# A scheduler that searches its priorities: 1,000 rounds of shifted keys, dearer key loads, and sums of w_in made early

## The chip, the cores and the metric

The kernel runs on one core of a Trainium2 chip. Its five engines each work through an instruction stream of their own: PE (TensorE: matmuls; PEld is its loading of weights), DVE (VectorE), ACT (ScalarE), POOL (GpSimd) and SP (SyncE), which here does nothing but issue DMAs. Streams wait for each other by semaphores. The metric is the device time of one execution in microseconds (us), the median of several runs.

## The reference

Sliding-window attention is followed by a two-layer network with a squared rectifier. There are B = 8 sequences of S = 576 tokens, H = 8 heads of D = 64, and a window of 32 tokens to either side:

```
scores = where(|i - j| <= 32, q k^T / 8, -1e9)
attn   = softmax(scores) v                      # (8, 8, 576, 64)
x      = attn, heads side by side               # (4608, 512)
h      = x @ w_in                               # w_in  (512, 2048)
out    = (s * relu(h)^2 + b) @ w_out            # w_out (2048, 512)
```

Everything comes in and goes out as float32; s and b are single numbers.

## The kernel before

**The work.** Attention goes through units of 128 keys. For each pair of heads PE makes the scores (L847), ACT takes the exponential (L875), DVE multiplies by the band mask (L879), PE multiplies by v (L905), and DVE divides by the sum (L927, L929) into a tile `xn`. PE (L936) or, from unit 24 on, a DMA (L953) turns `xn` into `XT`, the input of the first layer with its features on the partitions. One PE task, an attention step, holds the products with v of one unit and the scores of the next.

The first layer (`s1`) goes through blocks m of tokens (the first 512 tokens in m 0 to 2, the next 1024 in four blocks of 256, m 3 to 6, then m 7 to 12 of 512) and groups f of 128 hidden features. PE adds up 4 products per group into one of two banks `W` (L1192), ACT rectifies into a tile `r1` (L1199), and DVE squares two groups at once into `GT` (L1207). The second layer (`second`, L1358) works on 512 tokens at a time with seven products of half size in place of eight. For that DVE makes sums of the squares (`total`, L1350) and once, from w_out, four sums of weights (`weight_sums`, L1330). DVE combines the products into the output tiles (L1374), and SP stores them (L1383). The constant b is put in by way of column sums of w_out: PE makes four of them (`constant`, L1435, r = 0 to 3), one for each quarter of w_out, the last one once the last part of w_out is cast (L599).

For the last two full blocks of 512 tokens, 5 pairs of feature groups (features 6 to 15 of 16) use seven products too (`quad_group`, L1276). These need four sums each of w_in (L1239): `quad_sums` makes those of the first four pairs in the tiles `NAT` and those of the fifth in the tiles of the exponentials, all late.

**The packets.** From sequence 3 on, `later` loads q and k of a sequence as a packet of three parts (`piece`): q of 512 tokens (L773), k of 512 tokens in four DMAs (L780), and the tails, tokens 512 to 575 of both. They land in the ring `stg`, POOL (ACT for sequence 3) casts them into `nat` (L799), and a DMA that transposes turns them into QT and KT (L815). All of these DMAs are issued by SP, in one order with the loads of v (L624) and the stores. A packet waits for the attention step of an earlier unit (`paced`).

**The order.** Nothing of the order is written out by hand. Each `add` makes a task with a stream (an engine), a cost in ns, the resources that it reads and writes, and a `key`, its due time in us by a rough account (`P1`, `P2`, `due`). `_Graph.plan` then plays the program: at every step it takes the task that can start first by its account and, between equals, the one with the smallest key. A DMA has a weight; the rings of the queues are served in that account by these weights. The order in which `plan` started the tasks is the order of each engine's stream, and `emit` adds the waits. Tasks with keys below -100 (the first loads) keep the order in which they were made. A second, general program stands behind a flag for inputs whose exponentials leave the safe range; it isn't entered here.

Of the kernel before, what the change touches and what calls it, by code (L numbers as in the profile page):

```python
# [5 lines left out]
F32 = mybir.dt.float32  # L6
# [5 lines left out]
S = 576  # L12
# [49 lines left out]
HELD = 4  # L62
# [4 lines left out]
SUMS = ("dve", "dve")  # L67
STIR = {("turn", 0, "q"): 7, ("scores", 0): 3, ("turn", 1, "q"): 2, ("turn", 1, "k"): 1, ("turn", 2, "q"): 1, ("turn", 2, "k"): 1,
        ("turn", 3, "q"): 1, ("turn", 3, "k"): 1, ("scores", 2): 1, ("scores", 3): 1, ("av", 0): 5, ("turn", "t"): 2}
OUTSIDE = -1.0e38  # L70
# [20 lines left out]
class _Graph:  # L91
# [151 lines left out]

    def emit(self, sems):
# [91 lines left out]
def bass_sliding_window_symmetric__then__act_starrelu_kernel(  # L336
# [23 lines left out]
    with ExitStack() as es:  # L360
# [19 lines left out]
        NSTG, NNAT, NEX, NXN, NR1, NOUT, NVB, XR = 6, 6, 5, 5, 4, 5, 8, 1536  # L380
# [21 lines left out]
        SHUT = sb((128, 4, 128), BF16, "shut")  # L402
# [8 lines left out]
        TWICE = sb((128, 128), BF16, "twice")  # L411
        SPREAD = sb((128, 2 * 129), BF16, "spread")
# [6 lines left out]
        PART = sb((128, 128), F32, "part")  # L419
# [341 lines left out]
        def piece(b, parts, key, waits):  # L761
# [9 lines left out]
            for name, t0, n, p0 in parts:  # L771
                if name == "q":
                    fns.append(lambda e, t0=t0, n=n, p0=p0: e.dma_start(  # L773
                        stg[p0:p0 + n // 4, :].rearrange("p (h c) -> p h c", h=H),
                        q[b, :, t0:t0 + n, :].rearrange("h (p i) d -> p h (i d)", i=4)))
                    weight += n // 8 * 60.0
                    continue
                for i, c in enumerate(range(t0, t0 + n, 128)):
                    w = min(128, t0 + n - c)
                    fns.append(lambda e, i=i, c=c, w=w, p0=p0: e.dma_start(  # L780
                        stg[p0:p0 + w, DM * i:DM * i + DM].rearrange("p (h d) -> p h d", h=H),
                        k[b, :, c:c + w, :].rearrange("h p d -> p h d")))
                    weight += w // 2 * 21.5
# [427 lines left out]
        quad, weight = {}, {}  # L1211

        def quad_sums():
# [6 lines left out]
            for part, ft in enumerate(range(FASTEST, 16, 2 * HELD)):  # L1220
                n = min(HELD, (16 - ft) // 2)

                def piece_of(y, lower):
                    w = WIN_BF[:, 2 * lower:2 * lower + 2, 128 * ft:128 * ft + 256 * n].rearrange("p k (g y f) -> p k g y f", y=2, f=128)
                    return w[:, :, :, y, :]

                a11, a12, a21, a22 = (piece_of(y, lower) for y in (0, 1) for lower in (0, 1))
                if part == 0:
                    S, own = [NAT[i][:, :] for i in range(4)], [[("NAT", i)] for i in range(4)]
                else:  # L1230
                    S = [EXS[:, i * n // 4, :, :, :].rearrange("p h a c -> p (h a c)")[:, i * n % 4 * 256:] for i in range(4)]
                    own = [[("E", i * n // 4, hp, pr) for hp in (0, 1) for pr in range(NPAIR) if (4 * hp + pr) // (2 * n) == i % (4 // n)] for i in range(4)]
                    assert n in (1, 2)
                S1, S2, S3, S4 = S = [x[:, 0:256 * n].rearrange("p (k g f) -> p k g f", k=2, f=128) for x in S]
                Win = [("Win", i, x) for i in range(ft // 4, (ft + 2 * n - 1) // 4 + 1) for x in (0, 1)]
                for dst, a, b, op, reads, i in ((S1, a21, a22, ALU.add, [], 0), (S2, S1, a11, ALU.subtract, own[0], 1),
                                                (S3, a11, a21, ALU.subtract, [], 2), (S4, a12, S2, ALU.subtract, own[1], 3)):
                    eng = SUMS[part]
                    add(eng, lambda e, dst=dst, a=a, b=b, op=op: e.tensor_tensor(dst, a, b, op),  # L1239
                        510.0 * n if eng == "pool" else 140.0 + 141.0 * n,  # L1240
                        reads=Win + reads, writes=own[i], key=P1[NM - 2, ft] - AHEADS + 0.1 * i,
                        waits=[land["av", LONG, seq_units(LONG) - AFTER]])

                def of(view, res):
                    return lambda i, k: view[:, k, i, :], res

                weight[part] = {1: of(a11, Win), 2: of(a12, Win), 3: of(S4, own[3]), 4: of(a22, Win), 5: of(S1, own[0]),
                                6: of(S2, own[1]), 7: of(S3, own[2])}
# [11 lines left out]
        def quad_group(i):  # L1260
# [13 lines left out]
            def product(n, dst, first, k):  # L1274
                (lhs, lres), (rhs, rres) = weight[i // HELD][n], quad[n]
                add("pe", [lambda e, kk=kk: e.matmul(dst[1], lhsT=lhs(i % HELD, kk), rhs=rhs[:, kk, :], start=first and kk == 0, stop=(kk == 1),  # L1276
                                                     skip_group_check=True) for kk in (0, 1)],
                    c1(m) * 500.0, reads=lres + rres, writes=[dst[0]], key=k, slack=XTS if n < 3 else 0.0)
# [179 lines left out]
        for x in range(1, NG):  # L1458
            for m in BLOCKS[x]:
                attend(m)  # L1460
                for ft in range(0, 16 if x < NG - 2 else FASTEST, group(m)):
                    s1(m, ft)
            if x == NG - 2:
# [26 lines left out]
        g.plan()  # L1490
        streams = g.emit(sems)
# [230 lines left out]
```

## Time and profile before

| | us |
|---|---|
| median of 3 runs (302.62 to 304.06) | 303.09 |
| the profiled execution | 306.07 |
| its span, first to last instruction | 304.2 |

The profile's page names an engine's busy time, its share of the span and the number of its instructions. A row of the timeline reads: start in us, length in us, engine, line, operation, written tile <- read tiles, shapes, how many instructions in a row; in brackets stands the idle time ahead of it and what ended that. "SPq" rows are DMA issues, and last as long as SP was held by them. A chain row has only start, length and what. Matmul ends are modelled and overlap their successors by some 0.2 us.

### The profile page before, as it was taken

The page shows a single profiled execution, that of the slowest core. Times are in us where ns is not written, and L with a number is a line of the kernel's source. Part 1 is how long each engine was busy: PE and PEld are TensorE (multiplying, and loading weights), DVE is VectorE, ACT ScalarE, POOL GpSimd, SP SyncE. Part 2 cuts the span into 40 slices and gives each one's busy share as a digit, 9 for nine tenths or more (in the row PEclk, how much of TensorE's full clock was granted, in tenths as well). Part 3 has the DMA queues.
Part 4 walks back from the last instruction along what each step waited for, and adds up shares of the span by engine and source line. Part 5 has one row for each costly group of instructions (what it writes and reads, how often), then busy time and mean ns, then how long its engine had stood idle before and what let it go on. Part 6 is the DMA issues. An engine that isn't in the chain of part 4 may idle for free.

```text
span 304.2 us, 8852 instructions
## 1 busy us (share of the span) xinstructions
PE 292.3 (96%) x3839; PEld 210.0 (69%) x3839; DVE 238.9 (79%) x415; ACT 176.4 (58%) x277; POOL 64.1 (21%) x77
## 2 busy tenths in 40 slices
PE   8988999899999999999999989999999999999994
PEld 2457777688888887667766665665666666657883
DVE  5666888898779686977897888688898968879853
ACT  3856875685888664756465417554654576686000
POOL 5154577100000243034202800362000000000000
PEclk9999999999999999999999999999999999999999
DMA  6999999999892959999899969998922200121132
GB/s 211 303 256 322 303 293 367 266 252 255 188 196 82 255 119 176 235 251 188 130 289 202 155 152 234 241 184 191 209 71 71 84 3 32 37 69 36 46 114 91
DMA packets 118617, 54.44 MB, mean 179 GB/s; under 512 B 91232, under 2 KB 114400, under 8 KB 118576
## 3 DMA queue, kind: packets, MB, share of 16 engines
q1 hardware_dynamic: 118576, 53.85, 75.8%
q8 instruction: 31, 0.51, 0.8%
q14 instruction: 10, 0.08, 0.1%
HBM read 36.70 MB, written 9.44 MB: 152 GB/s over the span
## 4 chain that ended last, share of the span: by engine, by line
PE 64%; DMA 15%; SPq 5%; POOL 4%; issue 0%; DVE 0%; POOLq 0%
PE o L1358 29%; PE w L1192 22%; DMA stg<-in_moe_w_out_dram 6%; SPq L780 4%; DMA stg<-in_k_dram 4%; DMA kt<-nat 4%; PE avn L905 3%; POOL nat L799 3%; PE avn L1276 3%; DMA stg<-in_moe_w_in_dram 2%; PE sc L1358 2%; PE sc L1276 2%; PE sc L847 2%; PE avn L936 1%; PE w L1276 1%
## 5 line engine op out<-in xcount | busy, mean ns | idle before, releaser
L1192 PE MATMUL w<-xt,win 128*128 128x512 bf16 (+4 forms) x752 | 123.5, 307 | 0.7 <-issue 0.7
L1199 ACT ACTIVATE r<-w 128x512 bf16<-128x512 f32 (+2 forms) x126 | 73.1, 585 | 59.5 <-PE w L1192 59.0
L1192 PEld LDWEIGHTS w<-xt,win 128*128 128x128 bf16 x752 | 66.2, 98 | 29.3 <-issue 1.9
L1358 PE MATMUL o<-wout,gt 128*128 128x256 bf16 x512 | 64.3, 273 | 0.0
L1207 DVE TENSOR_TENSOR gt<-r 128x512 bf16<-128x512 bf16 (+3 forms) x84 | 50.6, 611 | 16.8 <-ACT r L1199 16.7
L1358 PEld LDWEIGHTS o<-wout,gt 128*128 128x128 bf16 x512 | 49.3, 98 | 12.3
L799 POOL CAST nat<-stg 128x1024 bf16<-128x1024 f32 (+2 forms) x28 | 32.8, 1173 | 82.2 <-DMA stg<-in_q_dram 65.2
L875 ACT ACTIVATE ex<-sc 128x1024 bf16<-128x1024 f32 (+1 forms) x29 | 29.7, 1023 | 14.9 <-PE avn L905 13.5
L1374 DVE SCALAR_TENSOR_TENSOR outs<-o,sb,cvec 128x512 f32<-128x512 f32 (+1 forms) x36 | 25.8, 718 | 9.7 <-PE o L1358 9.5
L1358 PE MATMUL o<-tw,gt 128*128 128x256 bf16 x256 | 32.2, 273 | 0.0
L1358 PEld LDWEIGHTS o<-tw,gt 128*128 128x128 bf16 x256 | 24.7, 98 | 5.9
L879 DVE TENSOR_TENSOR ex<-ex,mask 128x1024 bf16<-128x1024 bf16 (+1 forms) x29 | 22.5, 775 | 1.3 <-ACT ex L875 0.9
L1374 DVE SCALAR_TENSOR_TENSOR outs<-o,sb,outs 128x512 f32<-128x512 f32 (+1 forms) x27 | 19.4, 718 | 4.3 <-PE o L1358 4.2
L1350 DVE TENSOR_TENSOR gt<-gt 128x1024 bf16<-128x1024 bf16 (+1 forms) x24 | 22.1, 921 | 0.1
L929 DVE TENSOR_TENSOR xn<-avn,rec 128x512 bf16<-128x512 f32 (+1 forms) x31 | 21.2, 685 | 0.3
L905 PE MATMUL avn<-vb,ex 64*64 64x65 bf16 x944 | 19.9, 197 | 1.6 <-DMA kt<-nat 1.3
L905 PEld LDWEIGHTS avn<-vb,ex 64*64 64x64 bf16 x944 | 12.9, 106 | 10.6 <-issue 4.4
L1358 PE MATMUL o<-tw,gsum 128*128 128x256 bf16 x128 | 16.4, 273 | 0.0
L1358 PEld LDWEIGHTS o<-tw,gsum 128*128 128x128 bf16 x128 | 12.3, 98 | 3.4
L1350 DVE TENSOR_TENSOR gsum<-gt 128x1024 bf16<-128x1024 bf16 x16 | 12.2, 762 | 0.3
L632 ACT CAST vb<-vst 128x512 bf16<-128x512 f32 (+1 forms) x16 | 9.9, 616 | 3.9 <-DMA vst<-in_v_dram 3.9
L944 ACT COPY xt<-avn 128x512 bf16<-128x512 bf16 (+2 forms) x18 | 9.4, 530 | 4.2 <-PE avn L936 4.2
(188 smaller groups left out, 322.7 us busy)
## 6 DMA issues: line engine op xcount, KB each, us to landing
out_dram<-outs SPq DMA_DIRECT2D x32, 256.0 KB, 3.1
vst<-in_v_dram SPq DMA_DIRECT2D x28, 256.0 KB, 4.4
stg<-in_k_dram SPq DMA_DIRECT2D x24, 256.0 KB, 6.8
stg<-in_q_dram SPq DMA_DIRECT2D x5, 1024.0 KB, 6.6
stg<-in_moe_w_in_dram SPq DMA_DIRECT2D x8, 512.0 KB, 8.1
stg<-in_moe_w_out_dram SPq DMA_DIRECT2D x8, 512.0 KB, 8.0
stg<-in_q_dram SPq DMA_DIRECT2D x4, 512.0 KB, 8.6
stg<-in_k_dram SPq DMA_DIRECT2D x4, 512.0 KB, 8.4
```

Of the source, the lines that this page charges most:

```text
L799: (lambda e, dst=dst, src=src: e.tensor_copy(dst, src)),
L875: add("act", lambda e, dst=flat_dst, src=flat_src: e.activation(dst, src, AF.Exp, bias=0.0, scale=0.125), 190 + 0.833 * 512 * len(hs), rea ...
L879: add("dve", lambda e, flat=flat, mask=mask: e.tensor_tensor(flat, flat, mask, ALU.mult), 130 + 0.53 * 512 * len(hs), reads=[("E", ei, hp, ...
L905: return [lambda e: e.matmul(av[64 * x:64 * x + 64, h, 0:D + 1], lhsT=buf[64 * g:64 * g + 64, h % 2, h // 2, c:c + 64], rhs=VB[64 * g:64 * ...
L929: add("dve", lambda e: e.tensor_tensor(XN[xi][0:p1, :].rearrange("p (a c) -> p a c", a=H), av[0:p1, :, 0:D], REC[ri][0:p1, :].rearrange("p ...
L1192: add("pe", [lambda e, g=g, kc=kc: e.matmul(wt[:, g, :], lhsT=WIN_BF[:, kc, (f0 + g) * 128:(f0 + g + 1) * 128], rhs=XT[:, kc, t0 % XR:t0 % ...
L1199: add("act", lambda e: e.activation(rt, wt, AF.Relu, bias=0.0, scale=1.0), 190 + 0.833 * ng * nt, reads=[("W", wb)], writes=r1_res(rb, hal ...
L1207: (lambda e: e.tensor_tensor(GTS[gs][:, f1:f1 + nf, g0:g0 + nt], rr, rr, ALU.mult)),
L1276: add("pe", [lambda e, kk=kk: e.matmul(dst[1], lhsT=lhs(i % HELD, kk), rhs=rhs[:, kk, :], start=first and kk == 0, stop=(kk == 1), skip_gr ...
L1350: add("dve", lambda e: e.tensor_tensor(dst, x, y, op), 1240.0 if half is None else 690.0, reads=reads, writes=writes, key=k)
L1358: add("pe", [lambda e, g=g, j=j, dst=dst: e.matmul(dst, lhsT=lhs[:, g, 128 * j:128 * j + 128], rhs=rhs[:, g, :], start=first and g == 0 an ...
L1374: add("dve", lambda e, src=src, dst=dst, other=other: e.scalar_tensor_tensor(dst, src, SB128[:, 0:1], other, ALU.mult, ALU.add), 200 + 1.0 ...
```

## The change

Four things change.

- In `piece`, the weight of a DMA that loads k counts 25.0 in place of 21.5 for each two rows.
- After the first `plan`, a new method `improve` runs 1,000 rounds with a fixed seed. Each round shifts the keys of some tasks by a normally distributed amount (1.5 us standard deviation): all tasks of a kind, or those of a kind whose keys are near a drawn moment, or 30 tasks at random. It plans again and keeps the shift if the account's end is not later. Tasks with keys below -100 stay.
- The sums of w_in for the last three of the five pairs are made in a new tile SUMW once unit 9 of the long chain of units (sequences 3 to 7) has gone through its product with v, with a key in the middle of block x = 6; the first two pairs' sums are made late as before, in `NAT`.
- For the room, `xn` goes from 5 tiles to 3 and `r1` from 4 to 3, and SHUT, TWICE, SPREAD and PART, which serve the start, lie in SUMW.

```
-        NSTG, NNAT, NEX, NXN, NR1, NOUT, NVB, XR = 6, 6, 5, 5, 4, 5, 8, 1536
+        NSTG, NNAT, NEX, NXN, NR1, NOUT, NVB, XR = 6, 6, 5, 3, 3, 5, 8, 1536
...
-                    weight += w // 2 * 21.5
+                    weight += w // 2 * 25.0
...
+    def improve(self, rounds, seed):
+        draw = random.Random(seed)
+        mine = [t for t in self.tasks if t.key >= -100]
+        kinds = {}
+        for t in mine:
+            kinds.setdefault((t.stream, round(t.cost), len(t.fns), t.dma is None), []).append(t)
+        kinds = list(kinds.values())
+        best = max(t.fin for t in self.tasks)
+        for _ in range(rounds):
+            shift, some = draw.gauss(0, 1.5), draw.choice(kinds)
+            center, reach, way = draw.uniform(-30, 250), draw.choice((5, 15, 40)), draw.random()
+            if way < 0.4:
+                moved = [(t, shift) for t in some]
+            elif way < 0.8:
+                moved = [(t, shift) for t in some if abs(t.key - center) < reach]
+            else:
+                moved = [(t, draw.gauss(0, 1.5)) for t in draw.sample(mine, 30)]
+            old = [(t, t.key) for t, _ in moved]
+            for t, by in moved:
+                t.key += by
+            self.plan()
+            end = max(t.fin for t in self.tasks)
+            if end <= best:
+                best = end
+            else:
+                for t, key in old:
+                    t.key = key
+        self.plan()
...
+        SUMW = sb((128, 4, 256 * PAIRED), BF16, "sumw")
+        SHUT = SUMW[:, 0, 0:512].rearrange("p (i c) -> p i c", i=4)
...
+        def sums_of_w(ft, n, S, own, key, waits=()):
...
+            for dst, a, b, op, reads, i in ((S1, a21, a22, ALU.add, [], 0), (S2, S1, a11, ALU.subtract, own[0], 1),
+                                            (S3, a11, a21, ALU.subtract, [], 2), (S4, a12, S2, ALU.subtract, own[1], 3)):
+                add("dve", lambda e, dst=dst, a=a, b=b, op=op: e.tensor_tensor(dst, a, b, op), 140.0 + 141.0 * n,
+                    reads=Win + reads[:1], writes=own[i], key=key + 0.1 * i, waits=waits)
...
+            n = QUADS - PAIRED
+            weight[0] = sums_of_w(FASTEST, n, [NAT[i][:, :] for i in range(4)], [[("NAT", i)] for i in range(4)],
+                                  key - AHEADS, [land["av", LONG, seq_units(LONG) - AFTER]])
...
+            if x == 6:
+                weight[1] = sums_of_w(16 - 2 * PAIRED, PAIRED, [SUMW[:, i, :] for i in range(4)], OWNW, P1[BLOCKS[x][0], 8], [land["av", LONG, EARLYW]])
...
         g.plan()
+        g.improve(ROUNDS, SEED)
```

Here PAIRED is 3, EARLYW 9, ROUNDS 1000 and SEED 1.

More of the change, by code (lines that the diff above doesn't have):

```diff
@@ L61 @@
 TURNS = ("dve", "dve") * QUADS
-HELD = 4
+PAIRED = 3
+EARLYW = 9
 BYACT = [(y, x) for x in range(16) for y in (-1, -2)]
@@ L1219, in quad_sums @@
             T = [VST[:, i, :, :].bitcast(BF16).rearrange("p h d -> p (h d)").rearrange("p (k c) -> p k c", k=2) for i in range(4)]
[L1220 to L1248, printed above, removed]
@@ L1274, in product @@
             def product(n, dst, first, k):
[L1275 to L1276 removed]
+                (lhs, lres), (rhs, rres) = weight[i >= QUADS - PAIRED][n], quad[n]
+                add("pe", [lambda e, kk=kk: e.matmul(dst[1], lhsT=lhs(i if i < QUADS - PAIRED else i - QUADS + PAIRED, kk), rhs=rhs[:, kk, :], start=first and kk == 0, stop=(kk == 1),
                                                      skip_group_check=True) for kk in (0, 1)],
```

25 lines of the change are left out of this document (19 added, 6 removed).

## The prediction

> **What bounds the kernel now.** I start with the head of the profile's page, its busy line of TensorE, and the shares of the chain that ended last.
>
> ```profile
> span 304.2 us, 8852 instructions
> PE 292.3 (96%) x3839; PEld 210.0 (69%) x3839; DVE 238.9 (79%) x415; ACT 176.4 (58%) x277; POOL 64.1 (21%) x77
> PE 64%; DMA 15%; SPq 5%; POOL 4%; issue 0%; DVE 0%; POOLq 0%
> ```
>
> TensorE (PE) is busy 96% of the span. The change removes no matmul: both programs issue the same PE tasks, in another order. So only PE's idle time can be won, and the question is where that lies. The view by stretches, cut at the moments that matter below, answers it (columns: stretch, length, then busy us of PE, PEld, DVE, ACT and POOL, granted clock, DMA share, GB/s):
>
> ```profile
> 0.00:56.20 56.20, 50.53 (x854) 34.87 (x854) 38.73 (x88) 35.52 (x63) 30.63 (x47) 1.00 1.05 290
> 56.20:157.00 100.80, 100.06 (x1467) 78.29 (x1468) 83.25 (x141) 69.28 (x106) 16.49 (x16) 1.00 0.93 202
> 157.00:180.00 23.00, 22.06 (x288) 15.42 (x286) 19.46 (x29) 10.08 (x16) 8.21 (x7) 1.00 0.96 181
> 180.00:220.00 40.00, 39.46 (x515) 25.02 (x514) 32.02 (x48) 22.27 (x34) 8.75 (x7) 1.00 1.03 212
> 220.00:300.00 80.00, 79.93 (x721) 56.39 (x718) 65.00 (x111) 39.28 (x60) 0.00 (x0) 1.00 0.20 59
> ```
>
> Idle PE time is 5.67 us before 56.2, then 0.74, 0.94, 0.54 and 0.07 us. The granted clock is 1.00 throughout. The chain in order of time, and the timeline of PE and DVE, name the waits:
>
> ```profile
> 47.43 8.74 DMA stg<-in_moe_w_out_dram
> ...
> 56.19 0.71 DVE wout L599
> ```
> ```profile
> 56.94 0.40 PE L1435 MATMUL sc<-wout,onesw 128*32 128x512 bf16 x4 [0.83 <-DVE wout L599]
> 176.84 0.32 PE L905 MATMUL avn<-vb,ex 64*64 64x65 bf16 x16 [0.94 <-DMA kt<-nat]
> 212.62 0.32 PE L905 MATMUL avn<-vb,ex 64*64 64x65 bf16 x16 [0.33 <-DMA kt<-nat]
> ```
>
> The first wait is on the last part of w_out: it lands at 56.17 (47.43 + 8.74), DVE casts it, and PE's last column sum of w_out (L1435, r = 3) starts at 56.94. The DMA share up to there is 1.05: the loads come as fast as the engines move them, and the two programs issue them in the same order until after this one. So this moment is **pinned**: what PE saves before 56.9 it only waits longer, and the 5.67 us ahead of it can't be won. What can be won lies behind: 0.94 + 0.54 + 0.07 = 1.55 us, nearly all of it two waits for the keys (KT) of a later sequence, which L815 turns by DMA.
>
> **The change part by part.** The search moves almost every task, so I price it where PE waits or nearly waits. PE's tasks in question take, by the chain:
>
> ```profile
> 70.84 0.87 PE w L1192 x8
> 71.71 0.87 PE o L1358 x8
> 120.05 0.86 PE w L1192 x4
> ```
>
> *The w_out sum.* In before, PE has run the s1 groups up to f 10 of the 256-token block m 3 when it reaches the r = 3 sum. In after, the group f 10 stands behind the sum, and nothing else crosses it. Such a group is the row at 70.84, 8 matmuls in 0.87. The sum still can't start before 56.94, so PE leaves it with 0.87 us more work to do: **+0.87**. The bounds are 0 (the landing comes earlier by that much) and 0.87. Next comes the first product of w_out, which needs DVE's third weight sum: in before that ends at 60.96 and the product starts at 61.02.
>
> ```profile
> 59.74 1.22 DVE L1330 TENSOR_TENSOR wout<-wout,tw 128x2048 bf16<-128x2048 bf16 x1
> 61.02 1.05 PE L1358 MATMUL o<-wout,gt 128*128 128x256 bf16 x8
> ```
>
> In after PE has the same load between the sum and that product (three s1 groups in either order), so it comes there at the same time; nothing more is lost or won.
>
> *The later keys.* From the attention step that lets a packet's loads start (`paced`) to the first step that uses its KT, I counted PE's tasks in both orders. Sequence 4: the same 33 tasks. Sequence 5: one s1 group and one product fewer, 0.86 + 0.87 = 1.73 us less. Sequence 6: three s1 groups and one product more, 3 x 0.86 + 0.87 = 3.45 us more. Sequence 7, from the load of v that its packet stands behind: three s1 groups fewer, three products more, 0. So the heavier weight (25.0 for 21.5) gives one sequence of four more time, and takes it from another. What that means follows from when KT lands:
>
> ```profile
> 140.35 3.90 SPq L815 DMA_TRANSPOSE qt<-nat  x1
> 144.30 2.53 SPq L815 DMA_TRANSPOSE kt<-nat  x1
> 146.88 1.73 SPq L815 DMA_TRANSPOSE qt<-nat  x1
> 148.65 1.25 SPq L815 DMA_TRANSPOSE kt<-nat  x1
> ...
> 168.78 2.12 SPq L815 DMA_TRANSPOSE qt<-nat  x1
> ```
> ```profile
> 140.85 5.77 POOL L799 CAST nat<-stg 128x1024 bf16<-128x1024 f32 x5 [4.45 <-DMA stg<-in_k_dram]
> 150.89 0.32 PE L905 MATMUL avn<-vb,ex 64*64 64x65 bf16 x16
> ```
> ```profile
> 170.94 5.85 DMA kt<-nat
> 207.26 5.32 DMA kt<-nat
> ```
>
> Sequence 5's KT is issued at 144.30; with the 5.32 to 5.85 of the other two it lands at 149.62 to 150.15, and PE uses it at 150.89: 0.74 to 1.27 us to spare. With 1.73 us less, PE now waits 0.46 to 0.99 there. The order within the packet changes too: after loads the tails (tokens 512 to 575) first, and turns the q tail ahead of q and k. The bytes ahead of k are those that stood behind it, so all of them have landed when they had; the extra turn costs SP nothing if it fits before k's cast is done, and 1.73 if it doesn't. SP is free for it at 140.35 and k's cast starts at 140.85, so I take 0 and keep 1.73 for the range: **+0.7** (0.46 to 2.7). Sequence 6 waited 0.94; it has 3.45 us more, and pays for tails and one xt turn ahead of it (1.25 to 3 us by the two small turns above, one or both). **-0.94** (0 to -0.94). Sequences 4 and 7: **0** (up to 1.25, a small turn that now goes ahead of 4's KT); in 7 only the order of q and k is swapped, and both are needed at once.
>
> *Early sums of w_in.* Eight DVE instructions stay eight; their sums for three of the five pairs move from behind 220, where PE never waited, to both sides of the square of m 8's groups f 10 and 11, the one at 169.11 below. There POOL casts sequence 6's keys:
>
> ```profile
> 167.32 6.39 POOL L799 CAST nat<-stg 128x1024 bf16<-128x1024 f32 x5 [4.09 <-DMA stg<-in_k_dram]
> ```
> ```profile
> 164.52 0.69 DVE L1207 TENSOR_TENSOR gt<-r 128x1024 bf16<-128x1024 bf16 x1 [0.75 <-ACT r L1199]
> ...
> 169.11 1.52 DVE L1207 TENSOR_TENSOR gt<-r 128x1024 bf16<-128x1024 bf16 x1
> ...
> 171.73 1.52 DVE L1207 TENSOR_TENSOR gt<-r 128x1024 bf16<-128x1024 bf16 x1
> ```
> ```profile
> L1239 DVE TENSOR_TENSOR nat<-win x2: 685/686/687, 220.6 to 230.0; 128x1024 bf16<-128x1024 bf16 x2
> ```
>
> Four sums 768 wide, at three quarters of 686, are 2.1 us. DVE is busy 19.46 of the 23 us from 157 to 180, so 3.54 us are free and alone they would cost nothing. But a square takes 0.69 before the casts and 1.52 beside them, 0.83 more. If all four sums pay that, DVE needs 19.46 + 2.1 + 3.3 = 24.9 us: 1.9 too many. POOL has but five casts there, and the two squares pay already, so I let two sums pay: 23.2 us, 0.2 over, and PE is released late in bursts; I take **+0.5** (0 to 1.9). The Trainium skill, SBUF — State Buffer, section "SBUF: two separate sides", says that DVE's two-input instructions and GpSimd's share one port pair as an exclusive lock for a whole instruction. The trace agrees (1.52 against 0.69). By that rule every sum that meets a cast waits it out, and the sum goes to the 1.9 end: this is the second rival below.
>
> *Fewer buffers.* r1 goes from 4 to 3 and xn from 5 to 3; SHUT, TWICE, SPREAD and PART move into the new tile and are dead by then. With 3, a relu must wait for the square three groups back. The closest pair behind 62 us in before:
>
> ```profile
> 90.64 0.41 DVE L1207 TENSOR_TENSOR gt<-r 128x512 bf16<-128x512 bf16 x1
> ...
> 93.47 0.60 ACT L1199 ACTIVATE r<-w 128x512 bf16<-128x512 f32 x1
> ```
>
> The relu starts 2.4 us behind that square's end. That slack is the cover, and it goes only where DVE falls behind, as just priced. Cost **0**.
>
> *The tail.* After the last product both orders do the same:
>
> ```profile
> 299.17 1.04 PE L1358 MATMUL o<-tw,stg 128*128 128x256 bf16 x8
> 300.25 0.48 DVE L1374 SCALAR_TENSOR_TENSOR outs<-o,sb,cvec 128x256 f32<-128x256 f32 x1 [0.39 <-PE o L1358]
> ```
>
> The sum is 0.87 + 0.7 - 0.94 + 0.5 = +1.13, say +1.1 us: a profiled span of 305.3 for 304.2, its execution 307.2 for 306.07. The median of the runs shown, 303.09, is 3 us below that execution; the difference is carried over: **304.2 us**.
>
> **The rivals.**
> *The plan holds on the chip.* The search kept the order that ends soonest in its own account, so the waits for KT may all go: -1.55 + 0.87 = -0.7, 302.4 us. For it: sequence 6 does get 3.45 us. Against it: sequence 5 loses 1.73, and sequence 7 gains nothing. Were w_out to land earlier as well, 301.5; the DMA share of 1.05 speaks against that.
> *DVE becomes the bound at 160-180* (slower). All four sums meet casts: 1.9 us in place of 0.5, and sequence 5 waits its 1.0: +2.8, 305.9 us. It decides once DVE's work in that stretch passes 23 us; 19.46 + 2.1 is 1.4 short of it, which two blocked sums make good.
> *Sequence 5's keys come last* (slower). If the q tail's turn doesn't fit before k's cast, KT lands 1.73 later: +2.9, 305.9 us. For it: q's turn there took 3.90, on a queue still full of loads. Against it: the same turn took 2.12 for sequence 6.
> *It doesn't do what it says:* later keys get no more time. Half true by the counts, and the sum has it.
>
> **How the numbers follow.** The forecast has 0.42, with its own range of 303.3 to 305.2; the plan that holds 0.20, and with an early w_out 0.09; the DVE rival 0.14; the late keys 0.15. The range leaves out the early w_out and the worst of the slower two: 302.0 to 306.3. A measurement of this kernel can tell about 0.5% (1.5 us) from no change, so the borders are 301.6 and 304.6. Faster has the early w_out, 0.09; slower the two rivals, 0.29, and a third of the forecast, 0.14: 0.43; the same 0.48.
>
> **What would show it.** Right: in the profile after, the r = 3 sum still starts near 56.9, with a wait nearer 1.7 than 0.83 before it; the wait at sequence 6's first step is gone and one of 0.5 to 1 stands at sequence 5's, near 151; DVE shows no idle time from 165 to 180. Wrong: the sum starts before 56.2; PE's idle time behind it is below 1 us in all; or waits of over 1 us stand at places not named here, as at an xn buffer or a bank that DVE frees late.

## The result, and the profile after

After takes **307.25 us** (median of 4 runs, 306.67 to 307.74), before beside it 303.57 (302.62 to 304.30). The ratio is **1.0119, 95% interval 1.0085 to 1.0154**: slower, by about 3.7 us, where 1.1 was forecast. A later set of 6 runs of the same kernel (e9) gives 306.78 and 1.0102 (1.0059 to 1.0144). Every ratio here leaves out the slow runs of a kernel, those over 1.5% above its fastest, so it is not the quotient of the medians shown.

The profiled execution of after took 306.67 us, close to its median, while before's took 306.07, 2.5 over its own. The heads of the page of after, and its stretches at the prediction's cuts (columns as there):

```profile
span 304.9 us, 8836 instructions
PE 290.7 (95%) x3810; PEld 210.6 (69%) x3839; DVE 243.5 (80%) x415; ACT 177.0 (58%) x277; POOL 66.1 (22%) x77
PE 86%; DVE 5%; SPq 3%; DMA 2%; issue 2%; ACT 1%; POOL 0%
```
```profile
0.00:56.20 56.20, 50.09 (x840) 34.26 (x841) 40.21 (x87) 34.72 (x60) 31.33 (x47) 0.97 1.01 292
56.20:157.00 100.80, 98.73 (x1431) 77.80 (x1440) 84.56 (x139) 69.29 (x107) 17.09 (x16) 1.00 0.94 205
157.00:180.00 23.00, 22.50 (x280) 15.11 (x277) 21.53 (x34) 10.60 (x16) 9.44 (x7) 1.00 0.87 167
```

In the chain that ended last, DMA has gone from 15% to 2% and DVE has come from 0 to 5%. The granted clock of the first stretch is 0.97, where before had 1.00. Of PE's 3839 matmul records 29 are missing here (x3810), so PE's busy time reads low; its weight loads are all there, and places are read from them below.

The start, in PE's timeline and in stretches:

```profile
17.41 0.61 PE L711 MATMUL w<-onesw 128*128 128x512 bf16 x2
19.88 0.40 PE L759 MATMUL w<-ident,nat 128*128 128x128 bf16 x4 [1.86 <-POOL nat L745]
...
22.40 2.76 PE L1225 MATMUL w<-xt,win 128*128 128x224 bf16 x16
...
56.98 0.40 PE L1465 MATMUL sc<-wout,onesw 128*32 128x512 bf16 x4
```
```profile
17.80:21.20 3.40, 1.14 (x22) 0.75 (x24) 1.01 (x2) 1.19 (x4) 0.88 (x2) 1.00 1.10 273
21.20:24.60 3.40, 3.33 (x60) 2.62 (x61) 2.43 (x4) 2.52 (x5) 2.42 (x3) 0.50 0.96 241
```

PE idles 1.86 us for a cast of late rows of k, the clock is granted at half for the next 3.4 us, and 16 matmuls of 128x224 take 2.76 us, which take 1.70 at the full clock (e2, below). This belongs to the execution as much as to the order: in e9, the same kernel, the same wait is 0.41 us, in e8, with the same start, 0.80, and neither profile has a dropped clock. The fourth column sum of w_out still starts at 56.98, as before, but with no wait in front of it: what PE used to wait there it has lost earlier.

The largest wait behind that is at 112. POOL, DVE and PE of after:

```profile
105.14 5.85 POOL L832 CAST nat<-stg 128x1024 bf16<-128x1024 f32 x5 [12.93 <-DMA stg<-in_q_dram]
```
```profile
105.45 2.18 DVE L1240 TENSOR_TENSOR gt<-r 128x512 bf16<-128x512 bf16 x2
107.66 1.41 DVE L1380 TENSOR_TENSOR gsum<-gt 128x1024 bf16<-128x1024 bf16 x1
109.10 1.41 DVE L1380 TENSOR_TENSOR gt<-gt 128x1024 bf16<-128x1024 bf16 x1
110.43 0.83 DVE L1240 TENSOR_TENSOR gt<-r 128x512 bf16<-128x512 bf16 x1
...
111.41 0.69 DVE L962 TENSOR_TENSOR xn<-avn,rec 128x512 bf16<-128x512 f32 x1
```
```profile
112.16 0.40 PE L969 MATMUL avn<-ident,xn 128*128 128x128 bf16 x4 [1.16 <-DVE xn L962]
```

The same stretch of DVE in before, and POOL's casts there:

```profile
107.01 0.69 DVE L1350 TENSOR_TENSOR gsum<-gt 128x1024 bf16<-128x1024 bf16 x1
...
108.03 0.69 DVE L929 TENSOR_TENSOR xn<-avn,rec 128x512 bf16<-128x512 f32 x1
...
110.27 0.68 DVE L1350 TENSOR_TENSOR gt<-gt 128x1024 bf16<-128x1024 bf16 x1
```
```profile
103.88 2.22 POOL L799 CAST nat<-stg 128x1024 bf16<-128x1024 f32 x2 [11.67 <-DMA stg<-in_q_dram]
110.46 6.04 POOL L799 CAST nat<-stg 128x1024 bf16<-128x1024 f32 x5 [4.37 <-DMA stg<-in_k_dram]
```

In after POOL casts five tiles of sequence 4's packet in a row from 105. The two half sums (L1380) take 1.41 us each beside them. In before POOL stands still from 106.10 to 110.46, and the sums take 0.69 and 0.68. In after both sums also stand ahead of the xn that PE waits for; in before the xn stood between them. DVE shows no idle time from 102.96 to that xn. The Trainium skill, SBUF — State Buffer, section "SBUF: two separate sides", has the exclusive lock between DVE and GpSimd for this; the lengths here fit it: the 0.72 us more is less than one whole cast, 5.85 / 5 = 1.17 us.

No wait of PE for KT is left, at sequence 6 or any other.

To place the loss I take, for each task of PE, the median time to the next one over the profiles of before, e1 and after, add these up along the order, and subtract that work from the clock time. What is left is PE time lost until then, in us. It is an estimate, since it takes a task to cost the same in every order:

| until | e1 (before) | after | e9 (after) | e5 | e8 | e13 | e17 |
|---|---|---|---|---|---|---|---|
| 65 | 13.15 | 14.10 | 14.49 | 13.09 | 14.04 | 12.91 | 13.45 |
| 105 | 13.41 | 14.40 | 14.77 | 13.36 | 14.35 | 13.20 | 13.74 |
| 120 | 13.69 | 15.78 | 16.19 | 13.82 | 15.15 | 14.61 | 14.76 |
| 160 | 16.56 | 18.82 | 19.07 | 17.00 | 19.06 | 18.22 | 18.19 |
| 180 | 17.67 | 20.38 | 20.44 | 18.36 | 20.39 | 20.40 | 20.21 |
| 220 | 21.07 | 23.52 | 23.60 | 23.09 | 23.53 | 23.53 | 23.22 |

Against e1, a second profile of before, after loses 0.95 us more by 65, 1.1 between 105 and 120, and 0.45 between 160 and 180.

### The profile page after: what moved, and what is told of

It reads as the page before. It is cut to its first block, busy times and chain, and to the rows that moved or that the text cites. A ratio compares the mean times of both kernels' runs of the same rounds, so it can differ in the third digit from the quotient of the medians.

```text
span 304.9 us, 8836 instructions
## 1 busy us (share of the span) xinstructions
PE 290.7 (95%) x3810; PEld 210.6 (69%) x3839; DVE 243.5 (80%) x415; ACT 177.0 (58%) x277; POOL 66.1 (22%) x77
## 4 chain that ended last, share of the span: by engine, by line
PE 86%; DVE 5%; SPq 3%; DMA 2%; issue 2%; ACT 1%; POOL 0%
PE w L1225 34%; PE o L1388 33%; PE avn L938 4%; PE avn L1306 3%; DMA stg<-in_k_dram 2%; PE sc L880 2%; PE sc L1388 2%; DVE gt L1240 2%; PE sc L1306 2%; SPq L702 1%; PE avn L969 1%; SPq L672 1%; SPq L629 1%; DVE kt L751 1%; PE w L1306 1%
## 5 line engine op out<-in xcount | busy, mean ns | idle before, releaser
L1225 PE MATMUL w<-xt,win 128*128 128x512 bf16 (+4 forms) x726 | 118.2, 306 | 3.4 <-issue 1.9
L1232 ACT ACTIVATE r<-w 128x512 bf16<-128x512 f32 (+2 forms) x124 | 71.9, 585 | 64.8 <-PE w L1225 60.9
L1225 PEld LDWEIGHTS w<-xt,win 128*128 128x128 bf16 x752 | 66.9, 99 | 31.8 <-issue 2.0
L1240 DVE TENSOR_TENSOR gt<-r 128x512 bf16<-128x512 bf16 (+3 forms) x84 | 53.9, 653 | 16.2 <-ACT r L1232 16.1
L832 POOL CAST nat<-stg 128x1024 bf16<-128x1024 f32 (+2 forms) x28 | 34.1, 1218 | 82.2 <-DMA stg<-in_k_dram 46.9
L1380 DVE TENSOR_TENSOR gt<-gt 128x1024 bf16<-128x1024 bf16 (+1 forms) x24 | 22.6, 940 | 2.0 <-PE o L1388 1.7
L1380 DVE TENSOR_TENSOR gt<-gsum,gt 128x2048 bf16<-128x2048 bf16 x8 | 9.8, 1222 | 4.0 <-PE o L1388 4.0
L1380 DVE TENSOR_TENSOR gsum<-gt 128x1024 bf16<-128x1024 bf16 x16 | 11.9, 743 | 1.2 <-PE o L1388 1.0
```

The lines of the kernel that those rows point to most:

```text
L832: (lambda e, dst=dst, src=src: e.tensor_copy(dst, src)),
L1225: add("pe", [lambda e, g=g, kc=kc: e.matmul(wt[:, g, :], lhsT=WIN_BF[:, kc, (f0 + g) * 128:(f0 + g + 1) * 128], rhs=XT[:, kc, t0 % XR:t0 % ...
L1232: add("act", lambda e: e.activation(rt, wt, AF.Relu, bias=0.0, scale=1.0), 190 + 0.833 * ng * nt, reads=[("W", wb)], writes=r1_res(rb, hal ...
L1240: (lambda e: e.tensor_tensor(GTS[gs][:, f1:f1 + nf, g0:g0 + nt], rr, rr, ALU.mult)),
L1380: add("dve", lambda e: e.tensor_tensor(dst, x, y, op), 1240.0 if half is None else 690.0, reads=reads, writes=writes, key=k)
```

## The experiments

Each has its before beside it on the same chip; the ratio is to that. The chips differ: the medians of before are 303.83 (e1 to e4), 305.04 (e5 to e8), 303.38 (e9 to e12), 304.01 (e13 to e16) and 303.64 (e17, e18). So times of different sets are not to be compared.

| run | what | us | ratio (95%) |
|---|---|---|---|
| e1 | before itself | 304.40 | 1.0027 (0.9988 to 1.0065) |
| e2 | after, longer filler | 306.70 | 1.0104 (1.0055 to 1.0153) |
| e3 | after, start as before | 305.58 | 1.0070 (1.0038 to 1.0101) |
| e4 | after, no search | 305.43 | 1.0056 (1.0018 to 1.0094) |
| e5 | before, weight 25.0 | 305.89 | 1.0048 (1.0019 to 1.0078) |
| e6 | before, fewer buffers | 304.01 | 0.9990 (0.9959 to 1.0021) |
| e7 | before, search | 306.05 | 1.0033 (0.9997 to 1.0069) |
| e8 | after, one xn moved | 306.12 | 1.0019 (0.9983 to 1.0055) |
| e9 | after itself | 306.78 | 1.0102 (1.0059 to 1.0144) |
| e10 | after, casts on ACT | 313.37 | 1.0322 (1.0278 to 1.0367) |
| e11 | before, casts on ACT | 303.77 | 1.0009 (0.9980 to 1.0037) |
| e12 | before, weight 23.0 | 304.28 | 1.0025 (0.9997 to 1.0052) |
| e13 | after, s1 groups moved | 306.11 | 1.0056 (1.0022 to 1.0090) |
| e14 | e13 and two xn moved | 307.33 | 1.0106 (1.0054 to 1.0157) |
| e15 | before, later search alone | 303.85 | 0.9992 (0.9953 to 1.0031) |
| e16 | after, seed 2 | 306.23 | 1.0093 (1.0055 to 1.0131) |
| e17 | e14 and e2's filler | 306.54 | 1.0101 (1.0046 to 1.0157) |
| e18 | e15 and e2's filler | 305.04 | 1.0029 (0.9999 to 1.0060) |

**e1, before again.** No edit.

> The kernel before, unchanged, for a second profile of it. Its profiled execution took 306.07 us, 2.5 us over the median of its timed runs. Theory A (that profile caught late loads): spans here lie near 301.8 us, the wait of 0.83 us for w_out before 56.94 and the one of 0.94 for the keys of sequence 6 are smaller or gone, and the granted clock is 1.00. Theory B (the profile is typical and the profiler itself costs the time): the profiled span is again near 304.2 with both waits. Ratio 1.000 either way.

The span of this profile is 302.3, the execution 304.13 us, and the 12 runs reach from 302.34 to 306.44. The kernel against itself reads 1.0027, so a difference of 0.3 to 0.4% is about what such a comparison can't tell. Its stretches and the w_out sum:

```profile
56.20:157.00 100.80, 100.17 (x1468) 78.32 (x1469) 82.86 (x141) 69.18 (x107) 17.36 (x16) 1.00 0.93 207
157.00:180.00 23.00, 23.00 (x297) 16.39 (x296) 19.88 (x31) 9.87 (x16) 8.28 (x7) 1.00 0.92 176
180.00:220.00 40.00, 40.00 (x517) 25.18 (x514) 33.16 (x50) 22.50 (x35) 8.12 (x7) 1.00 1.00 211
```
```profile
56.84 0.40 PE L1435 MATMUL sc<-wout,onesw 128*32 128x512 bf16 x4 [1.07 <-DVE wout L599]
```

The waits of 0.94 and 0.33 us for KT are not there: PE is busy 23.00 of 23 and 40.00 of 40. They belonged to the one execution that the prediction had. The wait for w_out is there again. Theory A holds for the keys, B for w_out.

**e2, a longer filler.** The filler task of two matmuls at 17.43 us, made eight once the order is fixed:

```
+        land["stir", ("turn", "t")].fns *= 4
```

> The kernel after, with the filler task of two matmuls on ONESW that PE runs at 17.43 us made eight; no other instruction moves. After has PE idle for 1.86 us from 18.0 us, and the granted clock at half from 21.2 to 24.6 us. Theory C (the clock): half speed for 3.4 us costs 1.7 us; with PE busy there the clock stays at 1.00 and the time falls by 1.5 to 2.0, to 305.2 to 305.8 us. Theory D (w_out sets the end of the start, whatever PE does before it): the clock comes back and the time stays within 0.5 us of 307.25.

The clock is 0.999 to 1.000 in all 6 runs, and the ratio is still 1.0104. The 306.70 us are far from theory C's range and just outside D's 0.5 us, so D is the nearer one: the dropped clock is not what makes after slower than before. PE now waits a little later, for a part of w_in:

```profile
21.37 1.70 PE L1225 MATMUL w<-xt,win 128*128 128x224 bf16 x16
...
25.99 0.93 PE L1225 MATMUL w<-xt,win 128*128 128x224 bf16 x8 [0.97 <-POOL win L632]
```

and the first product of w_out starts at 61.41, against 61.02 in after. In this profile, what PE gains by the kept clock it waits for loads.

**e3 and e4, the start as before; no search.** e3 takes the shifts back where the first key is below 10; e4 has ROUNDS 0.

```
+        for t, key in zip(g.tasks, first):
+            if key < 10.0:
+                t.key = key
+        g.plan()
```

> The kernel after, with the search's shifts undone for the tasks with a first key below 10, so that the order up to about 61 us is that of before (fewer buffers, early sums, the heavier weight and the shifts of the later tasks stay). Theory C: no idle stretch at 18 us, clock 1.00, 305.0 to 305.8 us. Theory E (nothing but the start is worse): 303.3 to 303.9, the time of before. Theory F (the loss lies in the later order or the buffers): 306.5 to 307.3.

> The kernel after with no round of the search: fewer buffers, early sums and the heavier weight alone, with the start of before. Theory G (the search makes the loss): 303.0 to 304.0, that of before within 0.5 us, and no wait for an xn buffer or an r1 buffer above 1 us. Theory H (fewer buffers and early sums make part of it): 304.5 to 306.0, with waits of ACT's relu for DVE's square and of PE for xn beside POOL's casts.

1.0070 and 1.0056, both between before and after, and not told apart. So about half of the loss is there without any search: theory H by the time, but not by the waits that it named, of which e4 shows none (its longest behind 100 us is 0.7, for a square). e4 has the heavier weight too, which e5 takes alone. e3's 305.58 lies in theory C's range, and 10 of its 12 runs keep the clock; but e2 keeps it in all and gains little, so C's reason is not borne out. The rest of the loss comes with the search and, as e3 beside e2's 1.0104 suggests, with its order of the start. The wait for xn at 112 is in e3 too (0.9 us), and not in e4, with the same pools: the search's order makes it.

**e5, e6, e7, the parts alone, on before.**

```
e5:   weight += w // 2 * 25.0
e6:   NSTG, NNAT, NEX, NXN, NR1, NOUT, NVB, XR = 6, 6, 5, 3, 3, 5, 8, 1536
e7:   g.plan()
      g.improve(1000, 1)
```

> The kernel before with 25.0 for 21.5 in the account of a packet's key loads, and nothing else; the order of the start stays. The kernel after without its search ran 1.6 us (0.5 to 2.9) over before, and this tells which of its three other parts that is. Theory I (the heavier weight): 305.0 to 305.6 us, with waits of PE for KT or for v behind 120 us that before has not. Theory J (the buffers) and theory K (the early sums): 303.5 to 304.2, that of before.

> The kernel before with 3 r1 buffers for 4 and 3 xn buffers for 5, and nothing else. Theory J (the buffers make the 1.6 us): 305.0 to 305.6 us, and ACT's relu waits for a square of DVE three back, or DVE's xn for a transpose, at times when PE then idles. Theories I and K: 303.5 to 304.2, and no such wait is followed by PE's.

> The kernel before with the search of a thousand rounds, and nothing else (old weight, buffers and sums). Theory G (the search loses on the chip what it wins in its own account): slower than before by 1.3 us and more, 305.1 to 307.0, from the start (PE's lost time at 57 us 1 us over that of before) or from one place behind it where DVE is late. Theory L (the search is good and only the smaller pools make its orders slow): 301.5 to 303.5.

The buffers cost nothing (0.9990). The heavier weight alone costs 0.48%, theory I by the time, though it changes not one instruction, only the order. Its longest late wait, in POOL, DVE and PE of e5:

```profile
200.93 6.32 POOL L799 CAST nat<-stg 128x1024 bf16<-128x1024 f32 x5 [2.47 <-DMA stg<-in_k_dram]
```
```profile
205.25 1.52 DVE L879 TENSOR_TENSOR ex<-ex,mask 128x1024 bf16<-128x1024 bf16 x1
206.70 1.09 DVE L1207 TENSOR_TENSOR gt<-r 128x1024 bf16<-128x1024 bf16 x1
```
```profile
207.85 1.05 PE L1358 MATMUL o<-wout,gt 128*128 128x256 bf16 x8 [1.12 <-DVE gt L1207]
```

It is the pattern of after's 112 at another packet: a mask product doubled by POOL's casts stands ahead of the square that PE waits for. Theory I had waits for KT or v in its place, and there are none. The search alone gives 1.0033; its interval just reaches 1, so theory G is likely and not shown. In its trace PE has lost 14.65 us by 65 (e1 13.15) and 22.43 by 220 (e1 21.07): all of it is in the start.

**e8, the xn first.** The half sum at 109.10 (task 724) goes behind the xn at 111.41 (task 443) on DVE's queue.

```
+        for late, ahead in [(724, 443)]:
+            late, ahead = g.tasks[late], g.tasks[ahead]
+            g.order.remove(late)
+            g.order.insert(g.order.index(ahead) + 1, late)
```

> The kernel after with one instruction of DVE moved: the second half sum of w_out's columns of gt (L1380, at 109.10 us) goes behind the xn of sequence 3's unit 1 (L962, at 111.41), for which PE waits 1.16 us at 112.16; nothing else moves. Theory M (the order on DVE makes that loss): the wait goes, and the time falls by 1.0 to 1.4, to 305.9 to 306.3 us. Theory N (DVE is full there, and what stands behind is late instead): PE waits as long 2 to 10 us further on, and the time stays within 0.5 us of 307.25.

The wait at 112 goes, and comes back at 140, beside the casts of the next packet. DVE and PE of e8:

```profile
135.77 1.43 DVE L1380 TENSOR_TENSOR gsum<-gt 128x1024 bf16<-128x1024 bf16 x1
137.24 1.41 DVE L1380 TENSOR_TENSOR gt<-gt 128x1024 bf16<-128x1024 bf16 x1
...
139.24 0.68 DVE L962 TENSOR_TENSOR xn<-avn,rec 128x512 bf16<-128x512 f32 x1
```
```profile
139.98 0.40 PE L969 MATMUL avn<-ident,xn 128*128 128x128 bf16 x4 [0.98 <-DVE xn L962]
```

In after these two sums took 0.68 and 0.69 at 136.97, with no cast beside them. By 160 e8 has lost 19.06, after 18.82: theory N in the trace. The timed ratio, 1.0019, is below both of after's, and 306.12 lies in theory M's range. But the time doesn't bear this ratio out: e5, on the same chip and with the same runs of before beside it, has a lower median, 305.89, and a higher ratio, 1.0048. So a gain is not shown here, and e17 speaks against M.

**e9, after again.** No edit.

> The kernel after, unchanged, a second time beside the others. Its first four runs had all a dropped clock (0.993 to 0.994); e8, whose start is the same, dropped it in 4 of 12. Theory O (the drop is a matter of chance): about a third of the runs drop, and the ratio to before falls from 1.0119 to 1.006 to 1.009. Theory C again (after's start drops the clock each time): all runs near 0.994, ratio 1.0085 to 1.0154.

Only one of 6 runs has a mean clock of 0.994, against 4 of 4 at first, and the ratio is 1.0102. The drop is a matter of chance, as theory O has it, but the ratio did not fall below 1.01 with it, as in e2. That the drop costs nothing doesn't follow. The one run with a drop took 307.63, the other five have a median of 306.62, and in e3 to e8, e11 to e13, e15, e16 and before itself (last section) the runs at 0.994 or less are longer too, by 0.7 to 2.8 us. Whether the drop makes them so, or both come from late loads, was not separated.

**e10 and e11, the later casts on ACT.** e11 sets the engine before anything is planned. e10 moves the casts after the search and plans once more, with the priorities that were searched for POOL.

```
e11:
-CASTE = {"q": "pool", "k": "pool"}
+CASTE = {"q": "act", "k": "act"}
e10:
...
+        for task, fn, cost in land["swap"]:
+            task.stream, task.fns, task.cost, task.lat = "act", [fn], cost, g.LAT["act"]
+        g.plan()
```

> The kernel after with the key and query casts of the packets of sequences 4 to 7 (28 instructions of POOL at L832) moved to ACT, and the order made anew from the same priorities. Theory P (POOL's casts double what DVE runs beside them, and PE waits where the order puts too much on DVE there): no square takes 1.5 us behind 100 us, the wait for xn at 112 is gone, and the time falls by 1 to 2 us against after, to 1.000 to 1.005 of before. Theory Q (ACT is no freer): relu waits in ACT's queue behind 1.04 us casts, PE waits for r, and the ratio is 1.010 or more.

> The kernel before with the same 28 casts on ACT, and nothing else: the candidate for a version that beats both. Theory P: 0.992 to 0.998 of before, since no instruction of DVE behind 100 us is doubled any more. Theory Q: 1.003 to 1.010.

The doubling goes, and with it the wait at 112, though the xn still stands behind both half sums. DVE of e10:

```profile
107.06 0.69 DVE L1383 TENSOR_TENSOR gsum<-gt 128x1024 bf16<-128x1024 bf16 x1
107.79 0.69 DVE L1383 TENSOR_TENSOR gt<-gt 128x1024 bf16<-128x1024 bf16 x1
...
108.88 0.68 DVE L965 TENSOR_TENSOR xn<-avn,rec 128x512 bf16<-128x512 f32 x1
```

Theory P has the doubling right. The time still rises, to 2.1% over after's in e9: theory Q's ratio, but by a wait that neither theory had. DVE and PE of e10:

```profile
208.50 0.69 DVE L965 TENSOR_TENSOR xn<-avn,rec 128x512 bf16<-128x512 f32 x1 [1.90 <-DMA xt<-xn]
209.10 0.74 DVE L1407 SCALAR_TENSOR_TENSOR outs<-o,sb,cvec 128x512 f32<-128x512 f32 x1
209.76 0.68 DVE L915 TENSOR_TENSOR ex<-ex,mask 128x1024 bf16<-128x1024 bf16 x1
210.36 0.69 DVE L1243 TENSOR_TENSOR gt<-r 128x1024 bf16<-128x1024 bf16 x1
```
```profile
211.10 2.50 PE L1391 MATMUL o<-wout,gt 128*128 128x256 bf16 x16 [3.65 <-DVE gt L1243]
```

DVE waits for a transpose that still reads an xn tile. With three of them that cover is gone in this order. In e11, with five, the time stays (1.0009), neither P's gain nor Q's loss: either the doubled instructions cost before nothing, or the casts cost as much on ACT. e10 and e11 differ in more than the number of tiles, so that three tiles make the loss is argued from the wait. Behind it the clock is granted at half from 212.29 to 215.70, which lengthens the loss.

**e12, weight 23.0.**

```
-                    weight += w // 2 * 21.5
+                    weight += w // 2 * 23.0
```

> The kernel before with 23.0 for 21.5 in the account of the key loads, less than half of the step to 25.0, which cost 1.5 us (e5, ratio 1.0048). Theory I (more time for the keys is itself what costs): 1.001 to 1.003, and the later tasks move the same way as in e5. Theory R (any new order of DVE's work beside POOL's casts is a new draw): a ratio that does not lie between 1.000 and 1.005 in order, with PE's longest wait behind 100 us at another place than e5's 206 us.

1.0025, between, as theory I has it. The interval, 0.9997 to 1.0052, is too wide to exclude R, and the trace has R's sign: nothing waits at 206 us, and PE's longest wait behind 100 us is one of 0.46 for an xn, at 117.68.

**e13 and e14, moves on PE and DVE of after.** e13: the s1 group behind the fourth w_out sum goes ahead of it, and one more ahead of the first product. e14: also e8's move, and the two half sums of 135.77 behind the xn of 139.24.

```
e13:
+        for task, place, other in [(423, 'ahead', 306), (446, 'ahead', 474)]:
e14:
+        for task, place, other in [(423, 'ahead', 306), (446, 'ahead', 474), (724, 'behind', 443), (843, 'behind', 576), (844, 'behind', 843)]:
both:
+            task, other = g.tasks[task], g.tasks[other]
+            g.order.remove(task)
+            g.order.insert(g.order.index(other) + (place == "behind"), task)
```

> The kernel after with two s1 groups moved on PE's queue, and nothing else: the group that stands behind the fourth column sum of w_out (L1465, 56.98 us) goes ahead of it, and the next group of 256 tokens goes ahead of the first product of w_out, as in before. Theory S (the sum is pinned to w_out's landing, so work left behind it is lost): the sum starts within 0.6 us of where it did, and the time falls by 0.7 to 1.0 us, ratio to before 1.007 to 1.009. Theory D2 (PE comes to the sum late by itself in this order, so a group ahead of it only delays it): the sum starts 0.9 us later and the time stays, ratio 1.010 to 1.012.

> The kernel after with the moves of e13, that of e8 (xn at 111 us ahead of a half sum on DVE) and the same at 138 us: the two half sums (L1380) that stand ahead of the xn at 139.24 in e8 go behind it. Theory S and M together (the two places carry the loss): no wait for xn above 0.5 us, ratio to before 1.001 to 1.004. Theory N (each wait that goes is late at the next place): ratio 1.006 and more, with a wait of DVE's next packet in its place.

In e13 the sum starts at 56.69 with one more group done (theory S), and the loss at 65 is 12.91, near the 13.15 of e1, for 14.10 in after: the term is real. By 180 it is 20.40, as in after. PE of after, then of e13:

```profile
300.06 1.04 PE L1388 MATMUL o<-tw,stg 128*128 128x256 bf16 x8
```
```profile
163.09 0.83 PE L1388 MATMUL o<-wout,gt 128*128 128x256 bf16 x6 [0.95 <-issue]
...
300.06 1.04 PE L1388 MATMUL o<-tw,stg 128*128 128x256 bf16 x8
```

The last product starts at the same 300.06. On the way PE waits for xn again (twice, 1.5 us in all), and stands still for 0.95 us in the middle of a product for nothing that the profile shows. The time, 1.0056, is lower than after's by about half a per cent, a larger gain than theory S had. e14, which has the same moves and more, is at 1.0106, with all 6 of its runs at a dropped clock; its trace has no wait for xn above 0.4 us. So e13 speaks for a gain and e14 for none, and the intervals overlap.

**e15, the later search alone,** on before: the search, with the keys below 10 taken back as in e3.

> The kernel before with the search's keys of e7 for the tasks with a first key of 10 and more, and the start of before. In e7 PE lost 1.4 us more by 65 us than in before, and no more from there to the end. Theory T (only the search's start is bad): 0.998 to 1.001 of before, the candidate for a version that beats both. Theory R (every new order behind is a new draw): 1.002 to 1.008, with a wait of PE for DVE above 1 us somewhere behind 100 us.

0.9992: level with before. Theory T as far as the interval tells; no gain. With e7's 1.0033, and with e3 under e2, this points to the start as the place where the search loses, but none of these differences is clear of its interval.

**e16, another seed.** `ROUNDS, SEED = 1000, 2`.

> The kernel after with seed 2 for seed 1 in its search. Theory U (what ends sooner in the scheduler's account doesn't end sooner on the chip): 1.003 to 1.015 of before, with its waits at other places than after's. Theory V (seed 1 drew badly): 0.995 to 1.002.

1.0093, theory U. Its longest late wait is of a third kind, an output tile that DVE may not write until its store has gone. DVE and PE of e16:

```profile
204.13 0.75 DVE L1404 SCALAR_TENSOR_TENSOR outs<-o,sb,cvec 128x512 f32<-128x512 f32 x1 [3.58 <-DMA out_dram<-outs]
```
```profile
204.94 3.50 PE L1388 MATMUL o<-wout,gt 128*128 128x256 bf16 x16 [1.93 <-DVE outs L1404]
```

This wait is paid twice: behind it the clock is granted at half from 205.08 to 208.49, and the product takes 3.50 us, where one of the same form at 210.11 takes 1.91.

**e17 and e18, the filler added** to e14 and e15, as in e2.

> The kernel of e14 with the filler of e2 (eight matmuls for two). Theory S and M (work behind the w_out sum, and DVE's order at 111 and 138 us, carry the loss of the kernel after): with the clock kept, 1.001 to 1.005 of before, against 1.0104 for e2, which has the filler and none of the moves. Theory N (each wait comes back at the next place): 1.008 and more.

> The kernel of e15 with the filler of e2: the candidate for a version that beats both. Its clock should be 0.997 and more in all runs. If a dropped clock costs this order what it seemed to cost in e15 (306.3 against 303.5 us), the ratio to before is 0.995 to 0.999. If the start is bound by loads whatever PE does, it stays at 0.999 to 1.001.

e17 is at 1.0101, as e2 without the moves (1.0104): the two places, put right, give no gain that the times show (theory N). Two of its 6 runs dropped the clock all the same, and the interval, 1.0046 to 1.0157, just touches what theories S and M had. e18 at 1.0029 is above both of its ranges, with a drop in two of 12 runs, and no better than e15. No version here beats before.

## Why the prediction was wrong, point by point

**Two steps failed. The first is the base: the waits of one execution of before were priced, and its distance to the median was "carried over".** That execution took 306.07 us. Its 3 us over the median were taken for a fixed offset, and its wait of 0.94 us at sequence 6 for one that could be won. Both were chance: e1's profile of the same kernel took 304.13, and PE waits for no KT in it. So the term of -0.94 was not there to win.

**The second is that the sum prices the search only "where PE waits or nearly waits", which puts the new order of DVE's work beside POOL's casts at nothing.** In after this makes the wait of 1.16 us at 112, and 1.1 us of lost time between 105 and 120. The prediction had a wait of over 1 us at a place not named among its signs of being wrong, as at an xn.

Between the two profiled executions the change is worth 306.67 - 306.07 = +0.6 us. That this is near the +1.1 of the sum is luck, since it comes of a long execution of before. Against e1's execution it is 306.67 - 304.13 = +2.5, and the table places 0.95 + 1.1 + 0.45 of that; between the medians it is +3.7. The 1.2 us between the last two are the distances of these executions from their medians: e1's lies 0.56 above that of before, after's 0.58 below its own.

**The w_out sum, +0.87: about right in the trace, open in the time.** The sum starts at 56.98 (forecast near 56.9). The longer wait before it did not come, since PE came later by itself. e13, with one group put ahead of the sum and one ahead of the first product, has lost 1.2 us less than after by 65 (12.91 for 14.10). By 180 its trace has lost them again, to a second wait for xn and the stall of 0.95 us, and e14 and e17 show no gain in time.

**The later keys: wrong.** No PE waits for KT in after, so sequence 6's wait went as forecast; but e1 has none either, so nothing was won. Sequence 5's wait did not come. Its KT is issued at 143.32 for 144.30, and PE's first step with it, by the time PE reaches it, starts at 152.40 for 150.89:

```profile
143.32 2.15 SPq L848 DMA_TRANSPOSE kt<-nat  x1
```
```profile
152.40 0.32 PE L938 MATMUL avn<-vb,ex 64*64 64x65 bf16 x16
```

PE reaches it 1.5 us later, and KT is issued 1.0 us earlier. And the weight was costed by its keys only (-0.24 in all), where e5 measures +1.5 us (1.0048 of some 304). Its trace loses 1.3 us more than e1 between 180 and 220, where the wait of 1.12 at 206 lies; after loses no more there than e1 (3.14 for 3.40). So what the weight costs is a matter of the order that it meets, and e5's place is not after's.

**Early sums, +0.5: near in size, not in mechanism.** Two sums were to be lengthened by casts. In after they run at 171 to 175, behind the casts, and none is:

```profile
L1260 DVE TENSOR_TENSOR sumw<-win 128x768 bf16<-128x768 bf16 x2 | 1.1, 546 | 0.0
```

DVE is busy 21.53 of the 23 us from 157 to 180, what the sums alone add to before's 19.46 (2.1), and not the forecast 23.2. PE loses 0.45 more than in e1 between 160 and 180; that this is near 0.5 is luck, as far as the sums go. In e8 the first sum meets a cast and takes 1.39 us for 0.55, so it can come as forecast. e4 and e5 differ by 0.0008, so the times don't show the sums.

**Fewer buffers, 0: right** (e6), in this order. e10 shows where the cover goes.

**DVE as the bound:** the mechanism of this rival came true, its place did not. It was looked for at 160 to 180, where the sums went in, and was at 102 to 112, where only the order had changed.

**The clock of 1.00** did not hold in after's first runs. e2 and e9 show that this doesn't make the loss: with the clock kept, in all runs or in five of six, the ratio is 1.01 still.

**What stays open.** Weight alone 0.48% and search alone 0.33% come to 0.8%, inside e9's interval (from 0.59%) and just under that of the first runs (from 0.85%). That fits the two as the parts, but the search's own interval reaches 0, and the two were not run together without the rest. The places are not told: the wait at 112 and the group behind the w_out sum were put right (e17) without a gain in time, so that they make the loss is argued from the traces. e8 and e13 alone look better than the two together. Why after, e8 and e13 come to the same loss at 180 (20.38 to 20.40), from 14.40, 14.35 and 13.20 at 105, was not found, except that e13's stall is part of it.

## What to carry to other kernels

Profile the kernel before more than once, or compare its profiled execution with its timed runs, before pricing a wait of 1 us: here 1.3 us of waits for keys and most of the 3 us of offset belonged to one execution. A scheduler whose account gives each task one cost, whatever runs beside it, can be searched for a thousand rounds in its own terms and lose on the chip: after, e5 and e16 each have their longest late wait at another place (112, 206 and 204 us), where DVE is held up beside casts or by a store. Not every new order loses: e15's is level with before. When a wait is taken away, read the trace some 30 us further on before counting it (e8: 112, then 140).

## What the runs showed of the hardware

- PE was busy 1.14 of 3.40 us (17.8 to 21.2), with no idle stretch longer than 1.86 us, and the clock was granted at half for the next 3.4 us. The Trainium skill, TensorE: Matmul & The Clock Gate, section "HAM oscillation — how this bites in real kernels", gives as its rule no idle gaps above some 3.4 us; here the longest gap is about half that. In all ten profiles whose clock drops (after, e4, e7, e10, e12 to e16, e18) PE is busy for 1.16 (after) to 2.30 us (e14) of the 3.41 us ahead of the drop, so it took no single long gap. No threshold was measured.
- Of 132 runs of before beside the experiments, 26 had a mean clock of 0.994 or less, with a median of 304.9 us; the other 106 had 303.8.
- A wait of PE in the middle of the kernel can cost the clock too: 1.93 us in e16 and 3.65 in e10 are each followed by 3.41 us at half the clock.
- The same start drops the clock in some sets of runs and not in others: 4 of 4 (after), 1 of 6 (e9), 4 of 12 (e8), 6 of 6 (e14).
